# An attention and MLP kernel on one core: a longer software pipeline, a different split of the PSUM banks, and part of the MLP moved into the main loop

## The chip, the cores and the metric

The kernel runs on one core of a Trainium2 chip. The metric is the time on the device in microseconds (us), the median of several executions. TensorE appears in the profile as PE (matmuls) and PEld (weight loads), VectorE as DVE, ScalarE as ACT, GpSimd as POOL, and the queue that issues most transfers as SP.

## The reference

```python
xn = layernorm(x)                                  # x: 2048 tokens x 512
q = xn @ wq                                        # 32 query heads of 128
k, v = k_cache[:, :, -512:], v_cache[:, :, -512:]  # 8 groups, each for 4 query heads
p = softmax(q @ k.T * 128**-0.5)                   # per head 2048 x 512
s = concat(p @ v) @ wo                             # 2048 x 512
g = silu(silu(xn @ w1) @ w2)                       # MLP with 1792 hidden columns
out = x + s * g
```

Everything is bf16 and has to be accumulated in fp32.

## The kernel before

The 2048 tokens are four blocks of 512. The main loop has 128 steps, one for each pair of block and head. In a step TensorE does 4 score matmuls of head `s`, 4 query matmuls of head `s + 2`, 4 PV matmuls of head `s - LAG`, and some "fill": MLP work of later blocks while block 0 runs, then the output projection of the block before. A head passes through several engines: scores (PE), exp (ACT), normalisation (DVE), a transposing transfer of the probabilities into `pT` (SP and the DMA engines), PV (PE), eviction (DVE).

```python
LAG = 3            # PV runs this many steps behind the scores
OT_BUFS = 48       # buffers for head outputs waiting for the projection
LEAD = 8           # of two output tiles in work, the second is this many heads behind
PS_BUFS = {"sc": 4, "q": 1, "o": 1, "f": 2}   # PSUM banks by use, eight in both kernels

for s in range(NSTEP):
    # (cut: bookkeeping)
    score(s, 0)                        # matmul into an "sc" bank, exp into p_all
    if s >= 1:
        normalise(s - 1, 2, 3)         # DVE
        flip(s - 1)                    # transposing transfer p_all -> pT
    # query matmuls of head s+2 (bank "q"), with fill between them
    score(s, 1)
    # PV matmuls of head s-LAG (bank "o"), with fill between them
    score(s, 2)
    normalise(s, 0, 1)
    pump(cut[4])                       # fill: MLP or output projection (banks "f")
    score(s, 3)
    pump(cut[5])
```

A hidden tile of the MLP (`h_ps`, 4 matmuls) takes one "f" bank and is evicted by a tanh on ScalarE and then a multiply-add on VectorE. Before the loop block 0's MLP is done: 112 short hidden matmuls, then its 56 output matmuls (`oB_ps`). After the loop there is a tail that finishes the last block with products on combined operands (`m_ps`, 224 short matmuls).

The softmax here doesn't subtract the row's maximum and nothing guards it: scores larger than these inputs give would overflow.

## Time and profile before

| | before |
|---|---|
| median | 553.54 us (4 runs, 552.73 to 554.7) |
| span in the profile | 551.0 us |
| PE busy | 540.8 us, 98% |
| spacing of weight loads, 512-column matmul | 0.216 us |
| spacing of weight loads, 256-column matmul | 0.109 us |

First the engine table of the page: busy us, share of the span, instructions.

```profile
PE 540.8 (98%) x2628; PEld 260.8 (47%) x2676; DVE 460.9 (84%) x1263; ACT 388.3 (70%) x1122; POOL 20.5 (4%) x41
```

The chain that ended last, from the page, says the same:

```profile
PE 92%; DMA 4%; DVE 1%; ACT 1%; issue 1%
```

PE is the bound. How far is it from a floor? Its busy time can't tell. Matmul rows overlap (379 ns each, one every 216 ns), and their ends are modelled by the profiler, as the legend of the profile says. The starts of the weight loads are better, one for each matmul. 2312 long matmuls at 0.216 us and 336 short ones at 0.109 us make 536 us (worked out from these counts and spacings). So only a few us of holes exist, and I looked for them as spacings above the usual one.

The waits view of the kernel before, cut to the waits of PE that matter in the loop and to ACT's wait for the transposes (columns: total us, times, longest us):

```profile
ACT p_all L232 <- DMA pT<-p_all: 4.9, 7, 1.4
PEld L271 <- DMA pT<-p_all: 3.1, 6, 0.8
PEld L229 <- issue: 1.8, 5, 0.6
PE o_ps L271 <- DMA pT<-p_all: 0.3, 1, 0.3
PE h_ps L144 <- DVE hT L155: 0.3, 1, 0.3
```

There are two kinds of holes. Here is one of the first kind in the timeline of weight loads (start us, us, engine, line, operation, operands, count, idle before):

```profile
250.56 0.74 PEld L207 LDWEIGHTS <-wq 128*128 128x128 bf16 x4
251.42 0.10 PEld L229 LDWEIGHTS <-qT 128*128 128x128 bf16 x1
252.07 0.54 PEld L271 LDWEIGHTS <-v 128*128 128x128 bf16 x4 [0.55 <-DMA pT<-p_all]
```

```profile
250.78 1.03 PE L207 MATMUL q_ps<-xnT,wq 128*128 128x512 bf16 x3
251.64 0.38 PE L229 MATMUL sc_ps<-kT,qT 128*128 128x512 bf16 x1
252.08 0.82 PE L271 MATMUL o_ps<-pT,v 128*128 128x512 bf16 x3
```

PV waits for its transposed probabilities: 0.65 us between weight loads and not 0.216.

The second kind follows hidden matmuls. Both "f" banks are still waiting for tanh and multiply-add, and the next group may not start:

```profile
44.93 0.10 PEld L144 LDWEIGHTS <-w 128*128 128x128 bf16 x1
45.62 0.10 PEld L229 LDWEIGHTS <-qT 128*128 128x128 bf16 x1 [0.59 <-issue]
45.84 0.31 PEld L144 LDWEIGHTS <-w 128*128 128x128 bf16 x2
```

The profile says "issue" for the weight load, because what waits is a matmul. That matmul, at 45.62 us, is the last line of the waits view above.

### The profile page before, as it was taken

Reading aid. Unit: us, or ns where it says so; the run is one execution under the profiler, and the core shown is the slowest. Engines: PE = TensorE matmul, PEld = TensorE weight load, DVE = VectorE, ACT = ScalarE, POOL = GpSimd, SP = SyncE. Lnnn points to the kernel's source line nnn. Section 1 sums busy time; section 2 is a strip of 40 time slices with the busy share of each in tenths; the row PEclk is TensorE's granted clock in tenths of the full one; section 3 lists DMA queues with packets and bytes.
Section 4 is the critical chain, followed back from the end, with each engine's and each line's share of the span. In section 5 each row is a group of like instructions: output and inputs, shape, how many; then the busy total and the mean of one; then the engine's idle time right before and its main releaser. Section 6 shows DMA issues by size and latency. Waiting matters only on the chain.

```text
span 551.0 us, 8481 instructions
## 1 busy us (share of the span) xinstructions
PE 540.8 (98%) x2628; PEld 260.8 (47%) x2676; DVE 460.9 (84%) x1263; ACT 388.3 (70%) x1122; POOL 20.5 (4%) x41
## 2 busy tenths in 40 slices
PE   8999999999999999999999999999999999999996
PEld 5644444444444444444444444444444444444586
DVE  6888978967896688898889888988889889888887
ACT  5458667756775677777777777777788888788600
POOL 1000010000000000010001000100010001000010
PEclk9999999999999999999999999999999999999999
DMA  9748697886858899979797989897989887988931
GB/s 294 186 103 173 126 199 158 170 167 136 166 112 178 179 207 231 208 151 189 152 152 154 187 156 147 162 187 153 152 159 178 160 145 158 178 155 129 190 87 39
DMA packets 297837, 89.69 MB, mean 163 GB/s; under 512 B 282304, under 2 KB 296896, under 8 KB 297792
## 3 DMA queue, kind: packets, MB, share of 16 engines
q1 hardware_dynamic: 296064, 85.09, 80.6%
q0 software_dynamic: 1312, 3.67, 2.6%
q8 instruction: 21, 0.34, 0.2%
q10 hardware_dynamic: 416, 0.39, 0.2%
q14 instruction: 24, 0.20, 0.1%
HBM read 17.30 MB, written 2.10 MB: 35 GB/s over the span
## 4 chain that ended last, share of the span: by engine, by line
PE 92%; DMA 4%; DVE 1%; ACT 1%; issue 1%
PE o_ps L271 19%; PE sc_ps L229 19%; PE q_ps L207 19%; PE s_ps L328 14%; PE oB_ps L176 9%; PE h_ps L144 6%; PE m_ps L464 4%; DMA pT<-p_all 3%; PE h_ps L663 2%; ACT th L154 1%; ACT p_all L232 0%; DMA x<-in_A_x_dram 0%; DVE hT L155 0%; DVE st L108 0%; PE t_ps L627 0%
## 5 line engine op out<-in xcount | busy, mean ns | idle before, releaser
L232 ACT ACTIVATE p_all<-sc_ps 128x512 bf16<-128x512 f32 x512 | 305.1, 597 | 97.4 <-PE sc_ps L229 87.8
L229 PE MATMUL sc_ps<-kT,qT 128*128 128x512 bf16 x512 | 193.7, 379 | 0.7
L244 DVE TENSOR_SCALAR p_all<-p_all,rden 128x512 bf16<-128x512 bf16 x512 | 157.8, 351 | 9.1
L207 PE MATMUL q_ps<-xnT,wq 128*128 128x512 bf16 x501 | 135.0, 379 | 0.5
L271 PE MATMUL o_ps<-pT,v 128*128 128x512 bf16 x497 | 134.2, 379 | 1.0 <-DMA pT<-p_all 0.3
L277 DVE CAST oT<-o_ps 128x512 bf16<-128x512 f32 x128 | 88.3, 690 | 43.0 <-PE o_ps L271 40.6
L232 ACT ACTIVATION_READ_ACCUMULATOR p_all<-sc_ps 128x1 f32 x512 | 100.8, 197 | 0.0
L328 PE MATMUL s_ps<-wo_big,oT 128*128 128x512 bf16 x326 | 97.8, 379 | 0.5
L229 PEld LDWEIGHTS <-qT 128*128 128x128 bf16 x512 | 50.1, 98 | 61.6 <-issue 1.8
L219 DVE CAST qT<-q_ps 128x512 bf16<-128x512 f32 x112 | 77.0, 687 | 2.4 <-PE q_ps L207 2.4
L207 PEld LDWEIGHTS <-wq 128*128 128x128 bf16 x512 | 50.1, 98 | 61.0 <-issue 1.0
L271 PEld LDWEIGHTS <-v 128*128 128x128 bf16 x512 | 49.7, 98 | 61.5 <-DMA pT<-p_all 3.1
L176 PE MATMUL oB_ps<-w,hT 128*128 128x512 bf16 x215 | 62.6, 379 | 0.3
L328 PEld LDWEIGHTS <-oT 128*128 128x128 bf16 x384 | 37.6, 98 | 45.3
L144 PE MATMUL h_ps<-xnT,w 128*128 128x512 bf16 x165 | 51.5, 379 | 0.6 <-DVE hT L155 0.3
L242 DVE RECIPROCAL rden<-den 128x2 f32<-128x2 f32 x256 | 40.5, 158 | 10.3 <-ACT p_all L232 10.3
L155 DVE SCALAR_TENSOR_TENSOR hT<-th,h_ps 128x512 bf16<-128x512 bf16 x42 | 28.8, 685 | 7.2 <-ACT th L154 6.9
L176 PEld LDWEIGHTS <-hT 128*128 128x128 bf16 x224 | 21.9, 98 | 26.2
L154 ACT ACTIVATE th<-h_ps 128x512 bf16<-128x512 f32 x42 | 25.2, 599 | 6.5 <-PE h_ps L144 5.7
L144 PEld LDWEIGHTS <-w 128*128 128x128 bf16 x168 | 16.4, 98 | 20.0 <-issue 0.4
L185 ACT ACTIVATE th<-oB_ps 128x512 bf16<-128x512 f32 x16 | 9.5, 595 | 17.8 <-PE oB_ps L176 17.0
L345 POOL DMA_DIRECT2D out_dram<-x_e x12 | 6.6, 550 | 315.2 <-DVE rden L242 302.4
(63 smaller groups left out, 235.6 us busy)
## 6 DMA issues: line engine op xcount, KB each, us to landing
wq<-in_A_wq_dram SPq DMA_DIRECT2D x8, 512.0 KB, 4.1
w<-in_B_w_dram SPq DMA_DIRECT2D x3, 896.0 KB, 10.7
pT<-p_all SPq DMA_TRANSPOSE x128, 4.4
wo_big<-in_A_wo_dram SPq DMA_DIRECT2D x4, 512.0 KB, 4.5
x<-in_A_x_dram SPq DMA_DIRECT2D x3, 512.0 KB, 9.7
wo_big<-in_A_wo_dram SPq DMA_DIRECT2D x4, 384.0 KB, 4.2
x_e<-in_A_x_dram POOLq DMA_DIRECT2D x12, 128.0 KB, 3.1
out_dram<-x_e POOLq DMA_DIRECT2D x12, 128.0 KB, 2.2
```

The source lines that it names most:

```text
L144: nc.tensor.matmul(h_ps[:, lo : lo + n], w1_sb[f // FH][:, c, (f % FH) * P : (f % FH + 1) * P], xnT[b][:, c, lo : lo + n], start=(c == 0), ...
L154: nc.scalar.activation(th, h_ps, ACT.Tanh, scale=0.5)
L176: nc.tensor.matmul(cur["ps"], hT[b][f // 2][:, f % 2, j * P : (j + 1) * P], w2_sb[f // FH][:, f % FH, :], start=(f == 0), stop=(f == NFC - 1),
L207: nc.tensor.matmul(cur["ps"], wq_sb[h // REP][:, c, (h % REP) * DH : (h % REP + 1) * DH], xnT[b][:, c, :], start=(c == 0), stop=(c == ND - 1),
L219: nc.vector.tensor_copy(qT[s], cur["ps"])
L229: nc.tensor.matmul(sc, qT[s][:, j * P : (j + 1) * P], kT[h // REP], start=True, stop=True)
L232: nc.scalar.activation(p_all[s][:, :, j, :], sc.rearrange("p (kc q) -> p kc q", q=P), ACT.Exp, scale=INV_SQRT_DH, accum_out=den[s][:, j : ...
L242: nc.vector.reciprocal(rden, den[s][:, j0 : j1 + 1])
L244: nc.vector.tensor_scalar_mul(p_all[s][:, :, j, :], p_all[s][:, :, j, :], rden[:, j - j0 : j - j0 + 1])
L271: nc.tensor.matmul(cur["ps"], v_sb[h // REP][:, kc, :], pT[s][:, kc, :], start=(kc == 0), stop=(kc == NKC - 1))
L277: nc.vector.tensor_copy(oT[s // 2][:, s % 2, :], cur["ps"])
L328: nc.tensor.matmul(acc[j], oT[(b * HQ + h) // 2][:, h % 2, j * P : (j + 1) * P], wo_of(h), start=(h == 0), stop=(h == HQ - 1),)
```

## The change

The intent: give the transposes one more step before they are needed, give the MLP fill a third PSUM bank at the scores' expense, and take block 0's MLP output matmuls into the loop, where they fill the first steps, which have no PV yet. The rest pays for the memory or follows from these. The core of the diff:

```diff
-LAG = 3
-OT_BUFS = 48
-LEAD = 8
-PS_BUFS = {"sc": 4, "q": 1, "o": 1, "f": 2}
+LAG = 4
+OT_BUFS = 46
+LEAD = 4
+PS_BUFS = {"sc": 3, "q": 1, "o": 1, "f": 3}
@@ score, flip, out_units
-            p_all[s] = work.tile([P, NKC, BLKT, P], BF16, name="p_all", tag="p_all", bufs=3)
+            p_all[s] = work.tile([P, NKC, BLKT, P], BF16, name="p_all", tag="p_all", bufs=4)
-        pT[s] = work.tile([P, NKC, BLK], BF16, name="pT", tag="pT", bufs=3)
+        pT[s] = work.tile([P, NKC, BLK], BF16, name="pT", tag="pT", bufs=4)
     (cut: "sc" tiles get bufs=3, "f" tiles of the projection bufs=3)
@@ col_sums: VectorE sums of weights for the tail, a little later
-            s0 = 110 + 4 * i
+            s0 = (112, 116, 119, 122)[i]
@@ tail: four PVs are left and not three
-        for u in pv_units(NSTEP - 3):
+        for u in pv_units(NSTEP - 4):
     (cut: the others follow; one group of the tail takes an "f" bank)
@@ loads at the start: w2, x, wq, k, v in the order of their new use
+        load_kq(0)
     (cut)
@@ block 0's output matmuls
-        hs, os_ = mlp_units(0, lambda i: "f" if i % 3 == 2 else "sc")
-        for i, u in enumerate(os_):
-            u()
     (cut: statistics and queries of the first heads between them)
-        for b in range(1, NBLK):
+        for b in range(NBLK):
             hs, os_ = mlp_units(b, lambda i: "f")
-            fill += hs + os_
+            fill += hs * (b > 0) + os_
     (cut: fill spread over six places of a step; statistics and
      centring of the later blocks' x moved to other steps)
```

More of the change, by code (lines that the diff above doesn't have):

```diff
@@ L132, in flip_x, with load_kq @@
         nc.sync.dma_start_transpose(xnT[b][:, :, j * P : (j + 1) * P], x_blk[b][:, j, :])
-    def load_head_group(g):
+    def load_kq(g):
         nc.sync.dma_start_transpose(
@@ L138, in load_head_group, with load_v @@
         nc.sync.dma_start(wq_sb[g], wqv[:, :, g * REP * DH : (g + 1) * REP * DH])
+    def load_v(g):
         nc.sync.dma_start(
@@ L225, in score @@
         if j == 0:
-            p_all[s] = work.tile([P, NKC, BLKT, P], BF16, name="p_all", tag="p_all", bufs=3)
+            p_all[s] = work.tile([P, NKC, BLKT, P], BF16, name="p_all", tag="p_all", bufs=4)
             den[s] = work.tile([P, BLKT], FP32, name="den", bufs=3)
-        sc = ps.tile([P, W], FP32, name="sc_ps", tag="sc", bufs=4)
+        sc = ps.tile([P, W], FP32, name="sc_ps", tag="sc", bufs=3)
         nc.tensor.matmul(
@@ L326, in mm @@
             if h == 0:
-                acc[j] = ps.tile([P, D], FP32, name="s_ps", tag="f", bufs=2)
+                acc[j] = ps.tile([P, D], FP32, name="s_ps", tag="f", bufs=3)
             nc.tensor.matmul(
@@ L469, in f32pair @@
         def f32pair(name):
-            t = work.tile([P, 2, 2, HALF], FP32, name=name, tag="p_all", bufs=3)
+            t = work.tile([P, 2, 2, HALF], FP32, name=name, tag="p_all", bufs=4)
             return t[:, 0, :, :], t[:, 1, :, :]
@@ L520, in tail @@
         run(4, 0, EARLY)
-        for u in pv_units(NSTEP - 2):
+        for u in pv_units(NSTEP - 3):
             u()
@@ L524, in tail @@
             diag(p)
-        group(4, 1, "sc")
+        group(4, 1, "f")
         run(4, 1, EARLY)
+        for u in pv_units(NSTEP - 2):
+            u()
         for t in range(2):
@@ L610 @@
         nc.sync.dma_start(w1_sb[1], w1v[:, :, FH * P :])
+        nc.sync.dma_start(w2_sb[0], w2v[:, 0:FH, :])
+        load_kq(0)
+        nc.sync.dma_start(w2_sb[1], w2v[:, FH:, :])
         load_x(1)
-        for i in range(2):
-            nc.sync.dma_start(w2_sb[i], w2v[:, i * FH : (i + 1) * FH, :])
+        load_v(0)
         load_x(2)
         load_x(3)
-        load_head_group(0)
+        load_kq(1)
         warm_ps = ps.tile([P, BLK], FP32, name="warm_ps", tag="sc", bufs=PS_BUFS["sc"])
@@ L682 @@
                 keep(nc.vector, t3, 3)
-            if i >= 2 * FH - 5 and i % 2 == 1:
-                stats(1, (i - 2 * FH + 5) // 2)
-        stats(1, 2)
-        stats(1, 3)
-        hs, os_ = mlp_units(0, lambda i: "f" if i % 3 == 2 else "sc")
-        for i, u in enumerate(os_):
-            u()
-            if i == 2:
-                rstd_of(BLKT, BLKT)
-                for j in range(BLKT):
-                    center(1, j)
-                    flip_x(1, j)
-            if i % 4 == 3 and 1 <= i // 4 <= BLKT:
-                stats(2, i // 4 - 1)
-            if i == 20:
-                rstd_of(2 * BLKT, BLKT)
-            if i == 36:
-                for q in q_units(0):
-                    q()
-            if i == 47:
-                for q in q_units(1, "o"):
-                    q()
-        load_head_group(1)
         fill = []
-        for b in range(1, NBLK):
+        for b in range(NBLK):
             hs, os_ = mlp_units(b, lambda i: "f")
-            fill += hs + os_
+            fill += hs * (b > 0) + os_
         n_mlp = len(fill)
@@ L732, with spread @@
         sums = col_sums()
+        def spread(n):
+            cut = [n // 6] * 6
+            for k in (5, 4, 1, 3, 0, 2)[: n % 6]:
+                cut[k] += 1
+            return cut if n != 4 else (0, 0, 0, 0, 2, 2)
+        for i, tag in enumerate("qo"):
+            for u in q_units(i, tag):
+                u()
+            pump(3)
+        for j in range(BLKT):
+            stats(1, j)
+        rstd_of(BLKT, BLKT)
+        n_pre = done
+        n_more = 4 * LAG
         wo_first = False
@@ L738 @@
                 fill += out_units(b - 1)
-            n = (h + 1) * n_mlp // HQ - done if b == 0 else 4
-            cut = {4: (0, 0, 0, 0, 2, 2), 10: (2, 2, 2, 1, 1, 2), 11: (2, 2, 2, 1, 2, 2)}[n]
+            n = 4
+            if b == 0:
+                n = n_pre + min(4 * (h + 1), n_more) + (h + 1) * (n_mlp - n_pre - n_more) // HQ - done
+            cut = spread(n)
             qu = q_units(s + 2) if s + 2 < NSTEP else []
@@ L769 @@
                 sums.pop(0)[1]()
-            if 4 <= s < 4 + BLKT:
-                stats(3, s - 4)
-            if s == 4 + BLKT:
-                rstd_of(3 * BLKT, BLKT)
-            for b2, s0 in ((2, 3), (3, 11)):
+            for b2, s0 in ((2, 2), (3, 8)):
+                if s0 <= s < s0 + BLKT:
+                    stats(b2, s - s0)
+                if s == s0 + BLKT - 1:
+                    rstd_of(b2 * BLKT, BLKT)
+            if s < 2:
+                for j in (2 * s, 2 * s + 1):
+                    center(1, j)
+                    flip_x(1, j)
+            for b2, s0 in ((2, 7), (3, 14)):
                 if s0 <= s < s0 + BLKT:
@@ L777 @@
                     flip_x(b2, s - s0)
+            if s == 0:
+                load_v(1)
             if s % REP == 1 and s < HQ and s // REP + 2 < HKV:
-                load_head_group(s // REP + 2)
+                load_kq(s // REP + 2)
+                load_v(s // REP + 2)
             if not wo_first and done >= n_mlp - BLKT * NFC:
```

## The prediction

> **What bounds it now.** TensorE: 98% of the 551.0 us span (engine table), 92% of the chain of waits, granted clock 0.999. As PE busy time is modelled, I use the spacing of weight loads (their timeline): 0.216 us per 512-column matmul, 0.109 us per 256-column one, everywhere. [...] 2312 long matmuls cost 500 us, 336 short ones 37 us: a floor of 537 us between first transpose (5.7 us) and last matmul (546.7 us). The change leaves these counts alone; only holes can be won.
>
> **The holes** (spacing above the median, same timeline):
> - before the first h matmul, 2.8 us: untouched.
> - after score matmuls, where o_ps waits for transposed probabilities, 2.4 us (waits view: PE weight load <- DMA pT, 3.1 us, six times, at 72 to 480 us).
> - after h matmuls, the two f banks not yet evacuated (tanh, then VectorE, 0.6 to 0.7 us each), 1.7 us (40 to 46, 101 to 107, 140 to 146 us).
> - others, 0.3 us.
> So at most 4.4 us is to be won.
>
> **The change, costed.**
> 1. LAG 3 to 4, fourth pT and p_all: a transpose lands 4.4 us after issue (longest 6.9); now it has about two steps of 3.46 us less the normalisation. Another step covers 6.9 us. Wins about 2.3 us, and ScalarE's waits on pT (4.9 us, off the path).
> 2. A third f bank, taken from the scores (eight banks stay eight): wins about 1.4 us. Exp takes about 0.65 us of ScalarE per tile (estimate: ACT busy less its other groups, over 512); scores are 3 to 5 matmuls apart (0.65 us at the closest), so the third-last exp should be done. Cost up to 0.3 us.
> 3. Block 0's 56 output matmuls move into the steps; 16 fill the four steps without PV. PE work is the same. Block 0's steps grow from 22.5 to 23.6 matmuls; statistics pile up less on the h evacuations. wq0 is wanted at 20 us instead of 27.8; some 3.9 MB come before it, which at the 350 GB/s reached here land by 14 to 16 us. About 0. Risk: xnT1 must be there at 38 us; I expect 36.
> 4. LEAD 4, OT_BUFS 46: the first reused oT is free half a step before need, as before. 0.
> 5. Tail: one more PV and eviction in it, same counts. 0. The 4.3 us after the last matmul stay.
>
> **Prediction.** 3.7 of 4.4 us won: 553.5 - 3.7 = 549.8 us; 8 in 10 between 548.6 and 552.2. Faster by over 2%: 0.01; within 2%: 0.97; slower by over 2%: 0.02.
>
> **What would show it.** Step 1: PE <- DMA pT below 0.5 us. Step 2: excess after h matmuls below 0.4 us, and no new wait of scores on ScalarE. Step 3: q matmuls from 20 us without a gap, first h of block 1 near 38 us. Counts and pitch unchanged.
>
> **What would make it wrong.** A late wq0 or xnT1 (a hole of some us at 20 or 38 us); a VectorE backlog in block 0 (busy 4.9 of 5 us at 60 to 65 us) that stalls the single q or o bank; the three score banks stalling PE a little in each of 128 steps (0.05 us each would eat the gain); oT reuse missing its half-step margin.

The sum is 2.3 us for step 1 and 1.4 us for step 2, 3.7 us in all. The 350 GB/s of step 3 are from the trace of the kernel before: the core's transfers moved 366 GB/s from 5 to 10 us and 348 GB/s from 10 to 15 us.

## The result and the profile after

The changed kernel takes 550.21 us (median of 10 runs, 550.05 to 551.34); the kernel before took 553.36 us (15 runs, 552.6 to 554.7). The ratio is 0.9945, with a 95% interval of 0.9936 to 0.9954: about 3.0 us faster, well within 2%.

The engine table after:

```profile
PE 538.9 (98%) x2628; PEld 261.4 (48%) x2676; DVE 458.6 (84%) x1261; ACT 389.5 (71%) x1122; POOL 20.4 (4%) x41
```

The chain after:

```profile
PE 98%; DVE 1%; issue 1%; DMA 0%
```

The engine shares hardly move; the span went from 551.0 to 547.9 us with the same work. Nor does the share of the weight loads, 47% before and 48% after, show that holes have gone: a load takes 98 ns of each 216 ns with or without them. The chain tells more: DMA's 4% has gone. In the waits view no line of PE or ACT names `pT` any more. In the same step of the loop as above (with LAG 4 its PV is that of the head before), the weight loads now run without a hole; so do those of the same head's PV, one step later, from 252.44 us:

```profile
247.90 0.75 PEld L209 LDWEIGHTS <-wq 128*128 128x128 bf16 x4
248.77 0.10 PEld L231 LDWEIGHTS <-qT 128*128 128x128 bf16 x1
248.98 0.75 PEld L273 LDWEIGHTS <-v 128*128 128x128 bf16 x4
```

Nor is there one after hidden matmuls:

```profile
41.57 0.53 PEld L146 LDWEIGHTS <-w 128*128 128x128 bf16 x3
42.22 0.10 PEld L231 LDWEIGHTS <-qT 128*128 128x128 bf16 x1
42.43 0.53 PEld L146 LDWEIGHTS <-w 128*128 128x128 bf16 x3
```

To compare kernels I took three numbers from each one's timeline of weight loads. "After scores" and "after hidden" are the sums of the spacings above 0.216 us that follow a weight load of a score or a hidden matmul. The "stretch" runs from the first weight load after block 0's hidden tiles (at 19.4 to 19.9 us) to the last one of the program. It holds the same matmuls in every kernel.

| | after scores | after hidden | stretch |
|---|---|---|---|
| before | 2.42 us | 1.74 us | 526.58 us |
| changed | 0.03 us | 0.01 us | 523.35 us |

All holes of the stretch are gone, 4.36 us of them, counting another 0.2 us after query matmuls. Yet the stretch is only 3.23 us shorter. The reason lies in the fences of the section before. A weight load normally starts one matmul ahead of its own matmul: in both kernels every score matmul begins 0.213 to 0.215 us after its load. The load that waited until 252.07 us is only 0.01 us ahead of its matmul, at 252.08. So the first 0.2 us of its wait are covered by the matmul still running: the loads are 0.65 us apart there and the matmuls 0.44, and the next spacing of loads is 0.015 us. In the kernel before, seven spacings within the stretch and up to 515 us were shorter than 0.19 us, against one after; together they were 1.2 us below the usual spacing, against 0.1 us. That accounts for the 1.1 us. A hole after hidden matmuls is a real loss in full, because there the matmul waits: from 44.93 to 45.62 us loads and matmuls are both 0.69 us apart, and the next spacing of loads is 0.215 us.

### The profile page after: what moved, and what is told of

Its sections match the earlier page's. It is cut to its first block, busy times and chain, and to the rows that moved or that the text cites. A ratio compares the mean times of both kernels' runs of the same rounds, so it can differ in the third digit from the quotient of the medians.

```text
span 547.9 us, 8478 instructions
## 1 busy us (share of the span) xinstructions
PE 538.9 (98%) x2628; PEld 261.4 (48%) x2676; DVE 458.6 (84%) x1261; ACT 389.5 (71%) x1122; POOL 20.4 (4%) x41
## 4 chain that ended last, share of the span: by engine, by line
PE 98%; DVE 1%; issue 1%; DMA 0%
PE sc_ps L231 21%; PE q_ps L209 20%; PE o_ps L273 20%; PE s_ps L330 15%; PE oB_ps L178 9%; PE h_ps L146 7%; PE m_ps L466 4%; PE h_ps L669 2%; DMA x<-in_A_x_dram 0%; DVE st L108 0%; PE t_ps L633 0%; DVE x_t L594 0%; DVE m L490 0%; DVE xnT L638 0%; DVE x L122 0%
## 5 line engine op out<-in xcount | busy, mean ns | idle before, releaser
L178 PE MATMUL oB_ps<-w,hT 128*128 128x512 bf16 x219 | 64.7, 379 | 0.2
L146 PE MATMUL h_ps<-xnT,w 128*128 128x512 bf16 x165 | 49.5, 379 | 0.2
L188 DVE SCALAR_TENSOR_TENSOR gate<-th,oB_ps 128x512 bf16<-128x512 bf16 x16 | 11.0, 686 | 10.8 <-ACT th L187 10.8
```

The costliest lines, as they stand in the source:

```text
L146: nc.tensor.matmul(h_ps[:, lo : lo + n], w1_sb[f // FH][:, c, (f % FH) * P : (f % FH + 1) * P], xnT[b][:, c, lo : lo + n], start=(c == 0), ...
L178: nc.tensor.matmul(cur["ps"], hT[b][f // 2][:, f % 2, j * P : (j + 1) * P], w2_sb[f // FH][:, f % FH, :], start=(f == 0), stop=(f == NFC - 1),
```

## The experiments

Theory: the two kinds of holes are independent; the distance between transpose and PV closes the first, the third "f" bank the second, and the gains add up. Moving block 0's output matmuls is worth nothing by itself. Rivals: the extra buffers did it and not the distance; or the moved work cured block 0, where VectorE is nearly full (4.90 of 5 us at 60 to 65 us in the kernel before). All twelve runs gave correct results. Each had five rounds. The four runs of a call shared the kernel before on the same chip; its median was 553.76, 554.09 and 554.08 us in the three calls (the first and the third on one chip, the second, with a_l3_lead8, b_lead4, b_lag_nobuf and b_p4, on another).

| run | median us | ratio to before, 95% interval | after scores | after hidden | stretch us |
|---|---|---|---|---|---|
| b_lag | 552.30 | 0.9978 (0.9961 to 0.9995) | 0.00 | 2.37 | 525.69 |
| b_bank | 551.54 | 0.9962 (0.9946 to 0.9978) | 1.91 | 0.00 | 524.40 |
| b_lag_bank | 550.21 | 0.9938 (0.9923 to 0.9954) | 0.00 | 0.00 | 523.35 |
| a_lag3 | 554.14 | 1.0004 (0.9988 to 1.0020) | 5.26 | 0.00 | 527.56 |
| a_l3_lead8 | 551.91 | 0.9959 (0.9943 to 0.9976) | 1.84 | 0.00 | 524.05 |
| b_lead4 | 556.93 | 1.0043 (1.0028 to 1.0059) | 5.77 | 1.73 | 530.28 |
| b_lag_nobuf | 553.42 | 0.9986 (0.9970 to 1.0001) | 0.00 | 2.38 | 526.24 |
| b_p4 | 554.62 | 1.0004 (0.9989 to 1.0020) | 4.99 | 1.74 | 528.68 |
| a_bank | 552.94 | 0.9982 (0.9969 to 0.9994) | 0.00 | 2.82 | 526.13 |
| a_sc2 | 551.00 | 0.9947 (0.9933 to 0.9960) | 0.91 | 0.02 | 524.78 |
| b_nobuf_bank | 550.92 | 0.9945 (0.9933 to 0.9958) | 0.72 | 0.03 | 524.25 |
| a_pool | 548.98 | 0.9910 (0.9897 to 0.9924) | 0.07 | 0.02 | 523.35 |

The trace columns are from one execution each. Where a run is compared below with the changed kernel, 550.21 us, the two medians are of different calls. The ratios to before would give differences 0.7 us lower for a_lag3, a_bank, a_sc2 and b_nobuf_bank, mostly because the kernel before was slower in those calls than in that of the changed kernel. The spans of the traces agree better with the medians: 550.7 us in a_bank, 548.7 in a_sc2 and 548.8 in b_nobuf_bank, against 547.9 us. Names with b_ start from the kernel before, names with a_ from the changed one.

### Lag alone

```diff
-LAG = 3
-OT_BUFS = 48
-LEAD = 8
+LAG = 4
+OT_BUFS = 46
+LEAD = 4
 (and p_all, pT bufs=4, the tail's PVs, the later weight sums, as in the change)
```

> The kernel before with the longer lag alone (LAG 4, fourth pT and p_all, OT_BUFS 46, LEAD 4, the tail's extra PV), banks and block 0 as before. Theory (the lag removes the waits for transposed probabilities, and the gain is the net of those holes, about 1.5 us): 1.5 us faster, PE weight load <- DMA pT from 3.1 us to 0, the excess after h matmuls stays near 1.7 us. Rival (the waits in the loop are removed by the third f bank or the moved block 0 work, the lag does nothing): within 0.3 us of before.

It was 1.2 us faster, and no wait of PE on `pT` is left. The rival falls. The holes after hidden matmuls rose from 1.74 to 2.37 us, most of it by one of 0.58 us at 49.8 us that the kernel before has not. The timelines show what differs there. Step 3 has the first PV matmuls in the kernel before (48.64 and 49.50 us); at LAG 4 it has none yet, so its hidden matmuls come sooner after each other, and the one at 50.62 us waits for the eviction of a bank by VectorE. b_lag_nobuf, below, has the same hole. So with two "f" banks the lag takes away holes worth 1.5 us net (2.62 us less the 1.1 us that are covered) and opens 0.63 us of new ones; the stretch is 0.89 us shorter.

### Banks alone

```diff
-PS_BUFS = {"sc": 4, "q": 1, "o": 1, "f": 2}
+PS_BUFS = {"sc": 3, "q": 1, "o": 1, "f": 3}
 (and the same numbers where the tiles are made; one tail group on "f")
```

> The kernel before with the bank split alone (scores 3, f 3). Theory (the f banks alone make the holes after h matmuls): 1.7 us faster net, excess after h matmuls from 1.7 to below 0.2 us, PE <- DMA pT stays near 3 us. Rival (in block 0 VectorE is too full, because statistics, centring and h evictions meet there, and the moved block 0 work is what cures it): the holes at 40 to 46 us stay, and only those at 101 to 107 and 140 to 146 us go, 0.7 us faster.

It was 2.1 us faster (1.2 to 3.0 us by the interval), and all holes after hidden matmuls are gone, those at 40 to 46 us too. They were 1.74 us; most of the rest of the gain in stretch, 2.18 us in all, is that the holes after scores were 0.5 us smaller in this execution, which may be chance (b_p4 below shows how much they vary). PE's wait on `pT` stayed at 2.6 us. The rival, that only less VectorE work in block 0 could close the early holes, falls.

### Lag and banks together

```diff
 (both edits above on the kernel before; block 0's output matmuls stay before the loop)
```

> Lag and banks together on the kernel before, block 0 not moved. Theory: the two add, 3.1 us faster, equal to the changed kernel within 0.4 us, so the moved block 0 work is worth nothing. Rival (the block 0 move matters): 0.9 us or more slower than the changed kernel, with holes at 34 to 50 us.

Its stretch is the changed kernel's to the last digit, 523.35 us, and its median is the same 550.21 us. The two parts add up (1.2 + 2.1 us against 3.4 us by the ratios). The moved block 0 work, with its reordered loads and its new spread of fill, is worth nothing beside them.

### The changed kernel with the old lag

```diff
-LAG = 4
+LAG = 3
 (and the tail's PVs with it)
```

> The changed kernel with LAG 3 again, all else changed (four pT and p_all, three banks, block 0 moved). Theory: 1.5 us slower than the changed kernel (about 551.7 us), PE <- DMA pT back at 2 to 3 us at the places where the x and out transfers of the out-projection meet the transposes. Rival (the fourth buffers, not the lag, took the waits away): equal to the changed kernel, PE <- DMA pT near 0.

The rival falls: four buffers without the longer lag leave the waits in place. But it was a miss in size: it gave back 3.9 us and not 1.5, and was no faster than the kernel before. PE's wait on `pT` was far above that of the kernel before:

```profile
PEld L273 <- DMA pT<-p_all: 6.5, 8, 1.7
PE o_ps L273 <- DMA pT<-p_all: 2.6, 5, 1.2
```

So something else in the change makes the transposes later. To find it I followed heads through the timelines. Times are from the weight load of a head's last score matmul; the medians are over heads 40 to 119.

| us after the last score | before, median | before, head 47 | a_lag3, head 47 | changed, head 47 |
|---|---|---|---|---|
| exp done (ACT) | 1.23 | 1.23 | 1.23 | 1.23 |
| normalised (DVE) | 2.17 | 3.23 | 3.75 | 3.75 |
| transpose issued (SP) | 2.44 | 3.31 | 3.82 | 3.83 |
| landed | 6.91 | 9.24 | 9.90 | 10.25 |
| PV weight load | 8.85 | 9.28 | 9.95 | 12.30 |

From issue to landing a transpose (128 x 2048 bf16 elements) took 4.2 us at the least, 4.4 in the median and 6.9 at the most in the kernel before. At LAG 3 the median head has 1.9 us of slack between landing and PV, less than this spread, and head 47, like others at the end of an output tile, has none. Its transpose is issued later because VectorE is late, and then also takes about 6 us to land instead of the median 4.4, at a time when GpSimd issues a store of the output and two loads of `x` (245.6 to 248.0 us in the trace of before); no run tested these transfers by themselves. Four of the six waits in the kernel before are of this kind (heads 47, 63, 79 and 111). The other two are not. The transpose of head 5, at 73 us, is issued 3.6 us after its normalisation, because SP issues three loads for later heads first; that of head 113 is issued at 2.95 us but takes 6.85 us to land, with no transfer of the program beside it except transposes of other heads, and makes the longest hole, 0.70 us at 481 us. Why it lands so late is not known.

In a_lag3 VectorE is another 0.5 us late. The suspect was LEAD: two output tiles finish LEAD heads apart, and each costs VectorE a multiply and a multiply-add.

### The old lag with the old LEAD; LEAD 4 on the kernel before

```diff
 (a_l3_lead8: a_lag3 with)
-OT_BUFS = 46
-LEAD = 4
+OT_BUFS = 48
+LEAD = 8
 (and three pT, so that it fits in memory)
 (b_lead4: the kernel before with)
-LEAD = 8
+LEAD = 4
```

> The changed kernel with LAG 3, LEAD 8, OT_BUFS 48 and three pT (p_all four, banks and block 0 as changed). It follows a_lag3, which came out 3.9 us slower than the changed kernel and not 1.5. Theory (LEAD 4 puts the evictions of two finished out tiles, 1.4 us of VectorE each, into neighbouring steps, so the last normalisation before a transpose is 0.5 us later there, and at LAG 3 the transposes have no slack for it): excess after score matmuls falls from 5.3 us in a_lag3 to about 2.5 us, 1.5 us faster than a_lag3, about 552.5 us. Rival (the moved block 0 work or the score banks make LAG 3 worse): stays at 554 us.

> The kernel before with LEAD 4 alone. Theory (as above): the transposes at the ends of out tiles (about 246, 302, 357, 412, 468 us) land 0.5 us later relative to their PV, excess after score matmuls from 2.4 to 4 us or more, 0.5 to 1.5 us slower than before. Rival (LEAD is neutral, as the prediction had it): within 0.3 us of before.

Both bear the suspicion out. With LEAD 8 the holes after scores fell from 5.26 to 1.84 us and the time by 2.2 us (2.5 us by the ratios; the two runs were on different chips). That run also has `OT_BUFS` and the `pT` of before; b_lead4 changes LEAD by itself. LEAD 4 alone made the kernel before 2.4 us slower by the ratio, more than I expected. The timeline of VectorE in the kernel before, where an output tile ends:

```profile
243.36 0.62 DVE L244 TENSOR_SCALAR p_all<-p_all,rden 128x512 bf16<-128x512 bf16 x2
243.89 0.68 DVE L341 TENSOR_TENSOR sg<-s_ps,gate 128x512 f32<-128x512 f32 x1
244.60 0.69 DVE L342 SCALAR_TENSOR_TENSOR x_e<-sg,x_e 128x512 bf16<-128x512 f32 x1
245.21 0.16 DVE L242 RECIPROCAL rden<-den 128x2 f32<-128x2 f32 x1
245.41 0.62 DVE L244 TENSOR_SCALAR p_all<-p_all,rden 128x512 bf16<-128x512 bf16 x2
```

The tile before it was evicted at 236.98 us, two steps of 3.46 us earlier. In b_lead4 the second pair follows the first after 3.97 us:

```profile
241.79 0.68 DVE L341 TENSOR_TENSOR sg<-s_ps,gate 128x512 f32<-128x512 f32 x1
242.51 0.69 DVE L342 SCALAR_TENSOR_TENSOR x_e<-sg,x_e 128x512 bf16<-128x512 f32 x1
...
245.76 0.68 DVE L341 TENSOR_TENSOR sg<-s_ps,gate 128x512 f32<-128x512 f32 x1
246.48 0.69 DVE L342 SCALAR_TENSOR_TENSOR x_e<-sg,x_e 128x512 bf16<-128x512 f32 x1
247.09 0.16 DVE L242 RECIPROCAL rden<-den 128x2 f32<-128x2 f32 x1
247.28 0.62 DVE L244 TENSOR_SCALAR p_all<-p_all,rden 128x512 bf16<-128x512 bf16 x2
```

VectorE has not caught up from the first pair when the second comes, and the normalisation of head 47, the last line of each fence, ends 3.75 us after its last score and not 3.23. So LEAD 4 is a cost, and the longer lag hides it: in the changed kernel head 47 is just as late as in a_lag3 and its PV still waits for nothing. The smallest slack of any head there is 2.05 us. One hole of 1.2 us in b_lead4, at 231 us, is at no end of a tile, and b_p4 below has the same. It belongs to head 41, whose normalisation was on time (2.17 us), but whose transpose took 7.4 us to land (7.0 us in b_p4, 5.0 us in before). So LEAD is not behind this hole; whether more than chance is, one trace each can't tell.

### The lag without its buffers, and a buffer without the lag

```diff
 (b_lag_nobuf: the kernel before with)
-LAG = 3
+LAG = 4
 (and the tail's PVs and the later weight sums; p_all, pT bufs=3, OT_BUFS = 48, LEAD = 8 stay)
 (b_p4: the kernel before with)
-            p_all[s] = work.tile([P, NKC, BLKT, P], BF16, name="p_all", tag="p_all", bufs=3)
+            p_all[s] = work.tile([P, NKC, BLKT, P], BF16, name="p_all", tag="p_all", bufs=4)
```

> The kernel before with LAG 4 and nothing of its company: three pT, three p_all, OT_BUFS 48, LEAD 8 as before (the tail's extra PV is moved as it must be). Theory (only the distance between transpose and PV matters): PE <- DMA pT near 0, 1.2 us faster, as b_lag. Rival (the fourth buffers are needed for the lag): the transpose waits for the PV of the same step, about 2 us in, ScalarE's waits on pT rise over 10 us, and the holes after score matmuls stay; within 0.3 us of before, or slower.

> The kernel before with a fourth p_all alone, LAG 3. Theory: ScalarE's waits on pT (4.9 us) vanish, PE <- DMA pT stays near 3 us, the time stays within 0.3 us of before, as those waits are off the path. Rival (the waits of ScalarE delay the transposes): PE <- DMA pT falls under 1.5 us and 0.7 us or more is won.

With the lag alone all waits of PE on `pT` were gone, so the distance does it. The rival was right about ScalarE, whose wait on `pT` rose from 4.9 to 11.0 us, but that cost PE no more than 0.1 us of holes in the loop. The gain was smaller than b_lag's, 0.14% with an interval that just includes no gain. The stretch is 0.55 us longer than b_lag's, and one hole of 0.46 us among the PV matmuls at 515 us, in the last steps, is most of that; PV waits there for VectorE to empty its one bank, not for `pT`. With the buffer alone ScalarE's waits on `pT` vanished and nothing was won. The holes after scores, 5.0 us in this trace and 2.4 us in that of before, at equal times (ratio 1.0004), show how much single executions at LAG 3 differ.

### Lag and banks, with nothing else

```diff
 (the kernel before with LAG = 4 as in b_lag_nobuf, and the bank split of b_bank)
```

> The kernel before with LAG 4 and the new bank split alone: three pT and p_all, OT_BUFS 48, LEAD 8, block 0 not moved. Theory (distance and banks are all that counts): within 0.7 us of the changed kernel, about 550.7 us, the rest being a hole in the tail as in b_lag_nobuf. Rival (with three buffers ScalarE's waits hurt once the banks are split): 552 us or more.

As expected by the theory: 550.92 us, 0.7 us above the changed kernel, from holes of 0.33 us at 344 us and about 0.5 us at 511 to 514 us. The first is the rival's mechanism on a small scale: a transpose that landed 6.9 us after its issue kept its `p_all` buffer until 343.43 us, the exp that needed the buffer began at 343.53 us, 2.6 us after the weight load of its score and not 0.6, and a later score then waited for ScalarE. The fourth buffers with what pays for them are worth 0.7 us by the medians and 0.9 us of stretch, but nothing by the ratios (0.9945 for both kernels), so their worth is not settled.

### The old banks in the changed kernel

```diff
-PS_BUFS = {"sc": 3, "q": 1, "o": 1, "f": 3}
+PS_BUFS = {"sc": 4, "q": 1, "o": 1, "f": 2}
 (and the same numbers where the tiles are made; the tail group back on "sc")
```

> The changed kernel with the old bank split (scores 4, f 2), all else as changed. Theory (the third f bank closes the holes after h matmuls, wherever block 0's work lies): these holes come back, spacing excess after h matmuls 1.5 to 2.4 us, 1.7 us slower than the changed kernel, about 551.9 us. Rival (block 0's moved work, which spreads statistics and centring, would have closed most of them too): under 0.8 us slower.

It was 2.7 us slower than the changed kernel by the medians, more than either side expected, with 2.82 us of holes after hidden matmuls: five at 41 to 56 us, three larger ones at 96 to 107 us, three at 142 to 154 us. The rival falls. The kernel before had 1.74 us of them with the same banks. That a step of block 0 now carries 23.6 matmuls and not 22.5, so that two banks turn over faster, would explain more holes, but this is argued and not shown; b_lag, with the old fill, already had 2.37 us, for the reason given there.

### Two score banks

```diff
-PS_BUFS = {"sc": 3, "q": 1, "o": 1, "f": 3}
+PS_BUFS = {"sc": 2, "q": 1, "o": 1, "f": 4}
 (and the same numbers where the tiles are made; one more tail group and most of
  block 0's hidden tiles on "f")
```

> The changed kernel with only two score banks (scores 2, f 4; block 0's h tiles and one more tail group use the f banks). It asks how near three score banks are to costing something. An exp ends 1.2 us after its score matmul's weight load; with two banks a score waits for the exp two scores back, and the closest such pair is 6 matmuls, 1.3 us. Theory: it just fits in the steps without other ScalarE work and breaks where tanh or the query evictions on ScalarE come between: 0.5 to 2 us slower than the changed kernel, spacing excess in front of score matmuls. Rival (ample room): within 0.3 us of the changed kernel.

It was 0.8 us slower by the medians, but the stretch tells where: only 0.26 us of holes in the loop up to 510 us, 0.6 us in the last two steps, which have no query matmuls to space the scores, and 0.7 us in the tail, where the products wait for VectorE to empty a bank. These make the stretch 1.43 us longer, but the span only 0.9 us, because VectorE, which in the changed kernel is late at the end (next section), catches up meanwhile. So three score banks are far from costing anything, and even two nearly suffice. Half of my theory holds: it nearly fits. The two holes in the loop, 0.13 us each, do follow a tanh (at 87.96 and 174.42 us), but most of the loss is elsewhere, and none lies at the query evictions.

### A faster version

After the last matmul, at 543.61 us, the chain of the changed kernel still holds two evictions of output pieces:

```profile
540.99 2.63 PE m_ps L466 x24
543.62 0.41 DVE m L490
544.03 0.02 issue
544.05 0.42 DVE x_t L594
544.48 0.35 DVE m L490
544.82 0.02 issue
544.85 0.42 DVE x_t L594
```

Only one of the two pieces is made by the last matmuls. VectorE is 0.8 us late. One quarter of the tail's output can be finished elsewhere:

```diff
+        def finish_pool(r, c, v):
+            nc.gpsimd.tensor_tensor(out=v, in0=v, in1=g_of(r, c), op=ALU.mult)
+            nc.gpsimd.tensor_scalar_mul(v, v, 0.25)
+            nc.gpsimd.tensor_tensor(out=x_of(r, c), in0=v, in1=x_of(r, c), op=ALU.add)
+            store(r, c)          # the transfer to the output, as in finish
-        finish(1, 0, c21)
+        finish_pool(1, 0, c21)
```

> The changed kernel with one of the tail's four output quarters finished on GpSimd (three instructions) and not on VectorE (two, 1.4 us). After the last matmul VectorE has two output pieces left and not one, because it is 0.8 us behind. Theory: it catches up, the end after the last matmul falls from 4.3 to 3.5 us, 0.8 us faster than the changed kernel, about 549.4 us. Rival (GpSimd work slows VectorE beside it, or its quarter comes last): same or slower.

The chain now ends with one piece:

```profile
542.94 0.67 PE m_ps L466 x6
543.61 0.02 issue
543.63 0.43 DVE m L490
544.07 0.02 issue
544.09 0.42 DVE x_t L603
```

The rival's slower VectorE hardly shows: while the three GpSimd instructions ran (537.28 to 541.52 us), VectorE's took 0.68 to 0.69 us each, as in the changed kernel, except the multiply at 541.14 us, which took 0.93 us and not 0.69; whether GpSimd is behind that was not tested. The span fell from 547.9 to 547.1 us, as expected, and the end after the last matmul from 4.2 to 3.5 us. The median of 548.98 us is 1.2 us below the changed kernel's; the two medians are of different rounds, so the 0.8 us of the spans (547.0 to 547.2 us in its four runs, 547.8 to 549.0 in the ten of the changed kernel) is the safer figure for the theory. The rest lies outside the span: the time of a run is 1.8 to 1.9 us longer than its span here and 2.2 to 2.4 us in the changed kernel; why is not shown. The ratio to before is 0.9910. It is the fastest kernel.

## Why the prediction was right, point by point

- **The bound and the ceiling.** It said that counts and spacing stay and that only holes can be won, 4.4 us at most. Counts and spacing stayed (0.216 and 0.109 us), and all of these holes closed. But 4.4 us was too large a ceiling. It summed the excess of weight-load spacings, and in the waits for `pT` part of that excess is covered by the running matmul. The net was 3.2 us of stretch: about 1.5 us for `pT`, where 2.3 was forecast, and 1.7 us for the "f" banks, where 1.4 was. The two errors partly cancel, and so 549.8 us was forecast and 550.21 us measured, within the range.
- **Step 1, the lag, 2.3 us.** The mechanism was right: the wait of PE on `pT` is gone, and the lag without buffers does it too. The size was off: 1.5 us net of what the running matmuls cover, and 1.2 us for the lag alone by the ratio, as it opens a new hole where there are two "f" banks.
- **Step 2, the third f bank, 1.4 us.** Right: 1.74 us of holes are gone. Alone it gave 2.1 us, but the interval, 1.2 to 3.0 us, holds the forecast too. The estimate that three score banks cost up to 0.3 us was too careful; the excess after scores is 0.03 us.
- **Step 3, block 0's moved work, about 0.** Right, shown by b_lag_bank. wq0 landed at 14.7 us, as forecast, and the query matmuls began at 20.2 us without a gap. The first hidden matmul of block 1 came at 40.05 us and not 38, and the last piece of xnT1 landed at 38.8 us and not 36. The margin was thus 1.3 us, thinner than the forecast 2 us.
- **Step 4, LEAD 4 and OT_BUFS 46, 0.** Right in sum, but by luck: the reason was incomplete. It looked only at when a buffer comes free. LEAD 4 costs 2.4 us where the lag is 3, through VectorE and the transposes; the lag of the same change hides this cost.
- **Step 5, the tail, 0.** Right: the end after the last matmul stayed at 4.2 us. It said that these stay, and did not see that 0.8 us of them was VectorE's backlog.

## What to carry to other kernels

When the bounding engine is 98% busy, list its holes, and find for each the wait that ends it; here that told to 0.7 us what a change of many lines would win (3.7 us forecast, 3.0 us measured). Count a hole by the matmuls it delays and not by the weight load that waits, because the matmul still running can cover part of the latter, here 0.1 to 0.2 us of each of the six waits for `pT`. A pipeline distance is to be set for the worst item, here a head whose normalisation is late because an output tile is evicted beside it, or whose transpose lands late, and a parameter that looks neutral can be one that a longer distance merely hides.
